# Smaller weight loads, one tanh for two items, evenly spread projections and another start in a one-core attention and MLP kernel

## The chip, the cores and the metric

The kernel runs on one core of one Trainium2 chip. The metric is the device time of one execution in microseconds, as the median of repeated runs. PE is the matrix engine and PEld its weight load, ACT is ScalarE, DVE is VectorE, POOL is GpSimd, SP is the engine that issues the transfers.

## The reference

```python
xn = layernorm(x)                                  # x: 2048 tokens x 1024, bf16
qkv = xn @ wqkv                                    # 32 heads of 32
s = softmax(q @ k.T * 32**-0.5) @ v  -> @ wo       # attention branch
h = gelu_tanh(layernorm(xn) @ w1 + b1)             # w1: 1024 x 3584
g = silu(h @ w2 + b2)                              # w2: 3584 x 1024
out = x + s * g
```

## The kernel before

The attention is cut into 512 units: 8 groups of 4 heads, 8 query blocks of 256, 8 key blocks of 256. A unit is 8 score matmuls, two exps of 128x1024 on ACT, and the value and row-sum matmuls of two units earlier. The MLP (six chunks of at most 352 tokens) and the Q, K and V projections of the next head group are cut into items of about the size that fits into one unit, and each unit takes one item along. All items share one PSUM bank (bank 7), which DVE must empty before the next item can start. The scores have three slots of two banks, and each unit uses two of them, so PE can run ahead of ACT by less than one unit.

```python
while u < NU + 2 or ...:                   # the main loop, cut
    if u < NP: pro_unit(u)                 # the first 8 units: norm, transposes, first projections
    if u < NU: s_unit(u)                   # scores
    for t in act_tasks.pop(u, ()): t()     # tanh of earlier items
    if u < NU: exp_unit(u)                 # two exps
    if 2 <= u < NU + 2: pv_unit(u - 2)
    if u >= NP and state["qi"] < total:    # one item: W1, quarter of W2, K, Q or V
        ...
        for s in it.steps[lo:hi]: s(state["bank"])
        for t in dve_tasks.pop(u, ()): t()             # DVE work of earlier items
        if hi == len(it.steps): it.finish(state["bank"])   # DVE empties the bank
```

A W1 item leaves five operations behind: DVE empties the bank (`xb`), squares and multiplies one and two units later (`u`), and in the third unit ACT takes the tanh and DVE makes `hT`.

```python
            def fin(bk):                                   # w1_item, cut
                op("vector", ... tensor_scalar(xb, bank(bk), b1T ...))
                dve_tasks[u + 1].append(... ub = xb * xb)
                dve_tasks[u + 2].append(... ub = (ub + 1/0.044715) * xb)
                act_tasks[u + 3].append(... th = Tanh(ub))
                dve_tasks[u + 3].append(... hT[:, f] = (th + 1) * xb)
```

The weights come in pieces into two buffers. A W1 piece (4 items) is one transfer of 1 MB, a W2 piece two transfers of 0.75 and 1 MB.

```python
        def load_piece(g):                                 # cut
            s = g % 2
            if k < 7:
                op("sync", ... dma_start(w1v[s], src), w=[("war", s, 0)], dma=f"war{s}")
            else:
                op("sync", ... w2v[s][:, KLO:, :] ..., w=[("war", s, 1)], dma=f"wah{s}")
                op("sync", ... w2v[s][:, 0:KLO, :] ..., w=[("war", s, 0)], dma=f"war{s}")
```

At the start the tokens are taken in pairs of 128-token tiles. `pre_pair` holds the order of the work:

```python
        def pre_pair(p):
            more = p + 1 < NP
            if more: stat(2 * p + 2)       # statistics of a tile of the next pair
            nbias(p)
            xnorm(2 * p); xnorm(2 * p + 1)
            if more: stat(2 * p + 3); rstd(p + 1)
            ycoef(p)
            transp(2 * p); transp(2 * p + 1)
        def pro_unit(p):
            if p + 1 < NP: pre_pair(p + 1) # the next pair ahead of this pair's projections
            if p < 3: ynorm(p)
            pair_kq(p); pair_v(p)
```

The softmax here doesn't subtract the row's maximum and nothing guards it: scores larger than these inputs give would overflow.

## Time and profile before

| | before |
|---|---|
| median (three runs) | 1143.37 us (1141.6 to 1144.8) |
| profiled span | 1140.6 us |
| PE, ACT, DVE busy | 1091.3, 1053.7, 603.6 us |
| from the span's start to the first exp of unit 8 | 65.2 us |
| units 8 to 511 | 1028 us, 2.04 us each |
| after the last exp starts | 47.5 us |

These are lines of the page of before: the busy times, the chain that ended last, and three groups of operations (busy time and mean time of one; then the idle time of the engine just before them and what ended most of it).

```profile
PE 1091.3 (96%) x29952; PEld 695.6 (61%) x29952; DVE 603.6 (53%) x1351; ACT 1053.7 (92%) x1281; POOL 77.0 (7%) x128
...
PE 65%; ACT 27%; DVE 4%; DMA 2%; issue 1%; SPq 0%
...
L635 ACT ACTIVATE P<-ps 128x1024 bf16<-128x1024 f32 x1024 | 986.3, 1102 | 16.0 <-PE ps L623 12.4
...
L409 ACT ACTIVATE th<-u 128x352 f32<-128x352 f32 (+1 forms) x168 | 97.3, 579 | 0.3
```

Two engines are near their limit at once. How near is read from the starts in the timeline, not from busy times, since an ACT operation is shown as busy for longer than it holds up the next one (below, the tanh at 103.23 lasts 0.57 us, but the next exp starts 0.39 us after it). This is ACT in the timeline of before (start, duration, operation), in a stretch where W1 items and projections alternate:

```profile
103.23 0.57 ACT L409 ACTIVATE th<-u 128x352 f32<-128x352 f32 x1
103.62 3.85 ACT L635 ACTIVATE P<-ps 128x1024 bf16<-128x1024 f32 x4
107.23 0.61 ACT L409 ACTIVATE th<-u 128x352 f32<-128x352 f32 x1
```

One tanh and four exps take 4.00 us, two units; a tanh adds about 0.38 us to the 1.81 of two exps. PE needs 2.07 us for a unit with a W1, K or Q item and 1.77 with a V item. So four units W1, K, W1, V cost ACT 8.00 and PE 7.98.

Three kinds of lost time stand out. The first is the start. In the timeline of before, DVE has normalised tiles 0 and 1, and then waits for the rows of tile 4, although tiles 2 and 3 lie ready:

```profile
14.86 1.29 DVE L252 BATCH_NORM_STATS2 stats<-OT 128x6 f32<-128x512 bf16 x2 [3.00 <-DMA OT<-in_A_x_dram]
...
16.45 1.00 DVE L284 TENSOR_SCALAR hT<-OT,lnp 128x1024 bf16<-128x1024 bf16 x2
```

PE in the same stretch transposes tiles 2 and 3 after that, and only then starts the first projections (`xnT,wq`); the first scores (`QT,KT`) start at 23.11 us:

```profile
17.05 1.89 PE L306 MATMUL ps<-ident,hT 128*128 128x128 bf16 x16 [5.34 <-DVE hT L284]
18.87 2.56 PE L315 MATMUL ps<-xnT,wq 128*32 128x256 bf16 x64
21.26 1.92 PE L315 MATMUL ps<-wq,xnT 128*32 128x256 bf16 x64
23.11 0.40 PE L623 MATMUL ps<-QT,KT 32*128 32x256 bf16 x8
```

The second is PE standing still for about a microsecond in the middle of an item, with nothing in the profile that it could wait for ("issue"). The waits of PE between 65 and 1080 us of before (engine, what it was about to do, whom it waited for: total, times, longest):

```profile
PE ps L315 <- issue: 8.2, 11, 1.3
PE ps L315 <- DVE xb L401: 6.5, 15, 0.9
...
PE ps L652 <- issue: 1.6, 4, 0.6
PE ps L623 <- issue: 1.3, 2, 0.8
```

One of them in the timeline: a W2 item stops after 22 of its 28 matmuls.

```profile
186.28 1.06 PE L315 MATMUL ps<-hT,war 128*32 128x352 bf16 x22
188.31 0.48 PE L315 MATMUL ps<-hT,war 128*32 128x352 bf16 x6 [0.97 <-issue]
```

The third is a weight load near 960 us that stands in the queue behind the 2 MB of wo.

### The profile page before, as it was taken

The page shows a single profiled execution, that of the slowest core. Times are in us where ns is not written, and L with a number is a line of the kernel's source. Part 1 is how long each engine was busy: PE and PEld are TensorE (multiplying, and loading weights), DVE is VectorE, ACT ScalarE, POOL GpSimd, SP SyncE. Part 2 cuts the span into 40 slices and gives each one's busy share as a digit, 9 for nine tenths or more (in the row PEclk, how much of TensorE's full clock was granted, in tenths as well). Part 3 has the DMA queues.
Part 4 walks back from the last instruction along what each step waited for, and adds up shares of the span by engine and source line. Part 5 has one row for each costly group of instructions (what it writes and reads, how often), then busy time and mean ns, then how long its engine had stood idle before and what let it go on. Part 6 is the DMA issues. An engine that isn't in the chain of part 4 may idle for free.

```text
span 1140.6 us, 63237 instructions
## 1 busy us (share of the span) xinstructions
PE 1091.3 (96%) x29952; PEld 695.6 (61%) x29952; DVE 603.6 (53%) x1351; ACT 1053.7 (92%) x1281; POOL 77.0 (7%) x128
## 2 busy tenths in 40 slices
PE   4999999999999999999999999999999999899998
PEld 3756655566556665666666665666656565556666
DVE  7457661266672237665226675236585127752378
ACT  3889999999999999999999999999999999899930
POOL 4400000000000000000000000000000000000000
PEclk9999999999999999999999999999999999999999
DMA  9353245322245313224531236412134424443667
GB/s 222 76 169 123 61 114 174 117 80 78 62 129 149 109 43 114 74 72 130 149 104 41 76 107 196 142 61 77 41 105 125 144 90 142 150 133 116 114 172 174
DMA packets 198483, 129.90 MB, mean 114 GB/s; under 512 B 41552, under 2 KB 189008, under 8 KB 198224
## 3 DMA queue, kind: packets, MB, share of 16 engines
q1 hardware_dynamic: 193584, 125.85, 38.2%
q8 instruction: 234, 3.83, 1.4%
q0 software_dynamic: 4640, 0.02, 0.6%
q14 instruction: 25, 0.20, 0.1%
HBM read 104.87 MB, written 12.58 MB: 103 GB/s over the span
## 4 chain that ended last, share of the span: by engine, by line
PE 65%; ACT 27%; DVE 4%; DMA 2%; issue 1%; SPq 0%
PE ps L315 38%; ACT P L635 25%; PE ps L623 10%; PE ps L652 10%; PE ps L655 6%; ACT th L409 2%; DMA war<-in_B_w_dram 1%; DVE xb L401 1%; DMA OT<-in_A_x_dram 1%; DVE u L404 1%; PE ps L306 1%; DVE u L406 0%; DVE hT L413 0%; ACT thz L443 0%; DVE accs L666 0%
## 5 line engine op out<-in xcount | busy, mean ns | idle before, releaser
L635 ACT ACTIVATE P<-ps 128x1024 bf16<-128x1024 f32 x1024 | 986.3, 1102 | 16.0 <-PE ps L623 12.4
L652 PE MATMUL ps<-P,VP 128*32 128x256 bf16 x4096 | 264.1, 278 | 1.6 <-issue 1.6
L655 PE MATMUL ps<-P,ones 128*32 128x256 bf16 x4096 | 258.4, 273 | 1.8 <-issue 1.8
L315 PE MATMUL ps<-yTc,war 128*32 128x352 bf16 (+1 forms) x5376 | 226.6, 309 | 10.7 <-issue 5.1
L315 PE MATMUL ps<-hT,war 128*32 128x352 bf16 (+1 forms) x5376 | 230.1, 308 | 3.6 <-issue 3.1
L623 PE MATMUL ps<-QT,KT 32*128 32x256 bf16 x4096 | 204.6, 273 | 9.8 <-ACT P L635 5.6
L652 PEld LDWEIGHTS ps<-P,VP 128*32 128x32 bf16 x4096 | 108.2, 95 | 110.5 <-issue 98.0
L315 PEld LDWEIGHTS ps<-yTc,war 128*32 128x32 bf16 x5376 | 139.9, 97 | 58.4 <-issue 7.1
L315 PEld LDWEIGHTS ps<-hT,war 128*32 128x32 bf16 x5376 | 141.9, 97 | 45.3 <-issue 5.7
L401 DVE TENSOR_SCALAR xb<-ps,b1T 128x352 f32<-128x352 f32 (+1 forms) x168 | 96.0, 572 | 123.9 <-PE ps L315 122.9
L623 PEld LDWEIGHTS ps<-QT,KT 32*128 32x128 bf16 x4096 | 61.3, 93 | 155.9 <-ACT P L635 88.1
L315 PE MATMUL ps<-xnT,wq 128*32 128x352 bf16 (+2 forms) x3200 | 128.3, 304 | 2.3 <-DVE xb L401 2.1
L675 POOL TENSOR_TENSOR OT<-accs,rcs 128x256 bf16<-128x256 f32 x64 | 53.1, 830 | 1001.7 <-DVE rcs L673 1001.7
L440 DVE TENSOR_SCALAR zh<-ps,b2h 128x352 f32<-128x352 f32 (+1 forms) x48 | 27.5, 573 | 175.5 <-PE ps L315 175.5
L655 PEld LDWEIGHTS ps<-P,ones 128*32 128x32 bf16 x4096 | 110.3, 97 | 4.6 <-issue 3.4
L413 DVE SCALAR_TENSOR_TENSOR hT<-th,xb 128x352 bf16<-128x352 f32 (+1 forms) x168 | 85.7, 510 | 37.7 <-ACT th L409 34.9
L315 PEld LDWEIGHTS ps<-xnT,wq 128*32 128x32 bf16 x3200 | 79.9, 97 | 29.5 <-DVE xb L401 3.2
L409 ACT ACTIVATE th<-u 128x352 f32<-128x352 f32 (+1 forms) x168 | 97.3, 579 | 0.3
L404 DVE TENSOR_TENSOR u<-xb 128x352 f32<-128x352 f32 (+1 forms) x168 | 88.2, 525 | 0.2
L406 DVE SCALAR_TENSOR_TENSOR u<-u,xb 128x352 f32<-128x352 f32 (+1 forms) x168 | 82.9, 494 | 0.1
L315 PE MATMUL ps<-wq,xnT 128*32 128x256 bf16 x2048 | 65.9, 273 | 0.4 <-ACT xnT L309 0.3
L666 DVE COPY accs<-ps 128x256 f32<-128x256 f32 x64 | 27.2, 424 | 67.7 <-PE ps L655 67.7
(44 smaller groups left out, 497.1 us busy)
## 6 DMA issues: line engine op xcount, KB each, us to landing
war<-in_B_w_dram SPq DMA_DIRECT2D x66, 1024.0 KB, 5.6
war<-in_B_w_dram SPq DMA_DIRECT2D x24, 768.0 KB, 5.5
wq<-in_A_wqkv_dram SPq DMA_DIRECT2D x12, 512.0 KB, 5.9
OT<-in_A_x_dram SPq DMA_DIRECT2D x16, 256.0 KB, 6.6
y_scratch<-OT SPq DMA_DIRECT2D x16, 256.0 KB, 2.3
xnT<-in_A_x_dram SPq DMA_DIRECT2D x16, 256.0 KB, 4.1
out_dram<-wq SPq DMA_DIRECT2D x16, 256.0 KB, 2.7
gT_scratch<-gst SPq DMA_DIRECT2D x40, 88.0 KB, 1.7
```

What stands on the lines that cost most here:

```text
L315: ins = e.matmul(outs(j), lhsT=lhs(j), rhs=rhs, start=start, stop=stop, tile_position=(0, 32 * j), skip_group_check=True)
L401: op("vector", lambda e: e.tensor_scalar(xb[:, 0:n], bank(bk, 0, n), b1T[:, f:f + 1], None, op0=ALU.add), r=[("b", bk), "b1"], w=[kx])
L404: "vector", lambda e: e.tensor_tensor(ub[:, 0:n], xb[:, 0:n], xb[:, 0:n], op=ALU.mult), r=[kx], w=[ku]))
L406: "vector", lambda e: e.scalar_tensor_tensor(ub[:, 0:n], ub[:, 0:n], 1.0 / 0.044715, xb[:, 0:n], op0=ALU.add, op1=ALU.mult),
L409: "scalar", lambda e: e.activation(th[:, 0:n], ub[:, 0:n], ACT.Tanh, scale=0.7978845608028654 * 0.044715),
L413: "vector", lambda e: e.scalar_tensor_tensor(hT[:, f, 0:n], th[:, 0:n], 1.0, xb[:, 0:n], op0=ALU.add, op1=ALU.mult),
L440: op("vector", lambda e: e.tensor_scalar(zh[:, 0:n], bank(bk, 0, n), 0.25, b2h[:, nb:nb + 1], op0=ALU.mult, op1=ALU.add), r=[("b", bk), "b ...
L623: ins = e.matmul(bank(bks[j], kh * 256, (kh + 1) * 256), lhsT=KT[i2][32 * j:32 * j + 32, k0:k0 + 128], rhs=QT[i2][32 * j:32 * j + 32, qb * ...
L635: op("scalar", lambda e, p=p, sl=sl: e.activation(pb[:, 2 * p:2 * p + 2, :, :].rearrange("p a b q -> p (a b q)"), ps[:, sl * 1024:(sl + 1) ...
L652: e.matmul(bankq(ACC, j, 0, QW), lhsT=VP[vp][:, kb, vo + 32 * j:vo + 32 * j + 32], rhs=pb[:, j, kh, :], start=first, stop=False, tile_posi ...
L655: ins = e.matmul(bankq(ACC, j, QW, 2 * QW), lhsT=ones[:, 0:32], rhs=pb[:, j, kh, :], start=False, stop=last, tile_position=(0, 32 * j), sk ...
L675: op("gpsimd", lambda e: e.tensor_tensor(OT[:, hg, qb * QW:(qb + 1) * QW], a[:], rc[:], op=ALU.mult), r=[ka, kr], w=[("OT", hg, qb), ("xst ...
```

## The change

The change puts five things together. (1) Weight pieces are loaded in parts of 256 KB with a dependency each, handed to the queue one per unit. (2) Two W1 items share one tanh of 704 columns. (3) The projections are spread over the W1 items by a ratio, not strictly one after each. (4) At the start the rows and weights are loaded in another order, for the first two pairs the statistics come after the normalisation, and the transposes of the second pair come after the first projections. (5) The last multiplication of an attention block moves from POOL to DVE, one unit later.

```diff
-                op("sync", lambda e: e.dma_start(w1v[s], src), w=[("war", s, 0)], dma=f"war{s}")
+        def load_sub(g, q):
+            ...
+                dst, lo, hi = w1v[s], 2 * q, 2 * q + 2      # W2: 4 * q, 4 * q + 4
+            op("sync", lambda e: e.dma_start(dst[:, lo:hi, :], src[:, lo:hi, :]), w=[("war", s, q)], dma=f"war{s}{q}")
+        def load_piece(g):
+            ...
+            for i, q in enumerate(subs):
+                sp_tasks[cur["u"] + i].append((load_sub, g, q))
-                   r=[("war", s, 0), "yTc"], w=[("b", bk)])
+                   r=[("war", s, dc // 2), "yTc"], w=[("b", bk)])
@@ w1_item, fin
-                act_tasks[u + 3].append(... Tanh of th[:, 0:n] <- ub[:, 0:n])
-                dve_tasks[u + 3].append(... hT[:, f] ...)
+                gelu.append((xb, kx, f))
+                if h == 1:
+                    act_tasks[u + 3].append(... Tanh of th[:, :, 0:n] <- ut[:, :, 0:n])
+                    for i, (xq, kq, fq) in enumerate(pair):
+                        dve_tasks[u + 3].append(... hT[:, fq] ...)
@@ order of items
-                take_proj = need and len(flat) >= first_proj and (left - need < 6 or (w1_next and turn))
+                if need and len(flat) >= first_proj and (late or credit >= 1):
@@ start
-            if more:
+            if more and p >= 2:
                 stat(2 * p + 2)
             ...
             if more:
+                if p < 2:
+                    stat(2 * p + 2)
                 stat(2 * p + 3)
+            if 0 < p < NP - 1:
+                transp_pair(p + 1)
             pair_kq(p)
             pair_v(p)
+            if p == 0:
+                transp_pair(1)
@@ pv_unit
-                    op("gpsimd", lambda e: e.tensor_tensor(OT..., a[:], rc[:], op=ALU.mult), ...)
-                dve_tasks[v + 2].append(back)
+                dve_tasks[v + 3].append(lambda: op("vector", lambda e: e.tensor_tensor(OT..., a[:], rc[:], op=ALU.mult), ...))
```

(Cut: the load order at the start, the accounting of the ratio, and the buffers that go with the merged tanh: six `xb` instead of five, two double `u` instead of four single ones, one double `th` instead of two single ones.)

## The prediction

> **What bounds the kernel now.** ScalarE and TensorE are almost balanced. The page gives PE 96% and ACT 92% of 1140.6 us; from 95 to 900 us the window table shows both 98 to 99.8% busy. After a prologue of some 75 us come 504 attention units, each with one piece of MLP or projection work, about 2.04 us a unit. In the timeline the exps follow each other every 0.917 us, so 1.83 us a unit; a unit with a 352-column tanh takes 2.20. PE needs 2.07 us for a unit with a W1 or K/Q item, 1.77 with V, about 1.9 with a W2 part. So W1,K,W1,V costs ACT 8.01 and PE 7.98; W1,Q,W1,Q costs PE 8.28; W1 alone costs ACT 2.20; four W2 parts cost either about 7.7. The last 44 us are PE and DVE work that the change leaves alone.
>
> **1. One tanh for two items.** The Trainium skill ("ScalarE: Activation LUTs", What ACT_TABLE_LOAD costs) gives 186 ns + 0.833 ns per column for an ACTIVATE with immediates, 93 ns of it overlapped: 386 ns for 352 columns. The trace agrees (2.20 - 1.83 = 0.37). A pair would save about 0.09 us, 84 times: 7.5 us of ACT. Most is off the critical path: among projections PE already stands at 7.98. Only W1-only stretches (some 60 units) gain: 2 to 3 us. Against it, the two hT operations (0.44 us each) fall into one unit and wait for a longer tanh, in order ahead of the eviction of the single MLP bank; I estimate 0.1 to 0.3 us of PE wait in every fourth to eighth mixed unit: +3 to +5. POOL's multiplication (0.83 us, 64 times) becomes about 0.35 us each on DVE, 53% busy: little.
>
> **2. Even projections.** The item order shows small shifts: W1:projection goes from 1:1 to between 1:1 and 5:4; runs of Q stay. About 0. Six W1 items instead of four at the start, while DVE still normalises y: +1.
>
> **3. 256 KB parts.** Bytes stay. The chain shows a 12 us wait on a weight load behind the 2 MB of wo near 960 us, which cost ACT 3 to 4 us; finer dependencies should halve it. "Issue" waits of PE of up to 1.3 us (8.4 us on the MLP line) come near 1 MB bursts; W2 parts, freed unit by unit, may save some, W1 parts are still freed within one item. Together -3 to -6.
>
> **4. First token pair.** The chain shows 9.2 us waiting for x rows, until 14.86 us: statistics of tile 4 stand in DVE's order before the normalisation of tiles 2 and 3, and PE transposes these before the first projections. The change moves both and loads V after tiles 4 and 5. First scores should move from 23.1 to about 18 us, and PE's period of 5.5 us carries on: -4.
>
> **Sum:** about -7 us: **1136 us**, 8 in 10 within **1124 to 1147**. Faster by over 2%: 0.08; within 2%: 0.89; slower by over 2%: 0.03.
>
> **What shows it.** Right: first scores near 18 us; 84 tanh with a mean near 0.85 us; ACT busy down by 7 us without an equal fall of the span; more PE waits on DVE's evictions; shorter issue waits in W2 stretches. Wrong: mixed stretches clearly under 2.0 us a unit, or PE waits on DVE over 15 us.
>
> **What would make it wrong.** If buffers let PE or ACT run further ahead than I read, the full 7.5 us counts; if issue waits vanish, up to 10 us more; if bunched DVE work delays every bank, it is slower.

## The result, and the profile after

The changed kernel takes **1134.99 us** (median of four runs, 1134.89 to 1135.25) against 1144.09 us of before in the same rounds. The ratio is 0.9923, 95% interval 0.9905 to 0.9942. A ratio here is always the mean time of one kernel's fast runs over that of the other's of the same rounds, so not quite the ratio of the medians quoted. Between the two profiled runs the span fell by 7.4 us.

The page after, the lines that answer to those of before:

```profile
PE 1093.9 (97%) x29952; PEld 687.1 (61%) x29952; DVE 613.9 (54%) x1415; ACT 1048.2 (92%) x1197; POOL 24.0 (2%) x64
...
PE 63%; ACT 25%; DVE 9%; DMA 2%; issue 1%; SPq 1%
...
L676 ACT ACTIVATE P<-ps 128x1024 bf16<-128x1024 f32 x1024 | 971.5, 1087 | 19.5 <-PE ps L664 11.6
...
L431 ACT ACTIVATE th<-u 128x704 f32<-128x704 f32 (+1 forms) x84 | 66.7, 794 | 0.0
```

ACT is busy for 5.5 us less, but DVE's share of the chain went from 4 to 9%. The start did what was meant: in the timelines of DVE and then of PE, the normalisation of tiles 2 and 3 comes at 12.62 us and the first scores at 18.79.

```profile
12.62 1.00 DVE L285 TENSOR_SCALAR hT<-OT,lnp 128x1024 bf16<-128x1024 bf16 x2
13.54 1.28 DVE L253 BATCH_NORM_STATS2 stats<-OT 128x6 f32<-128x512 bf16 x2
```

```profile
11.34 3.61 PE L316 MATMUL ps<-xnT,wq 128*32 128x256 bf16 x64 [1.27 <-ACT xnT L310]
15.52 2.34 PE L316 MATMUL ps<-wq,xnT 128*32 128x256 bf16 x64 [0.57 <-DMA wq<-in_A_wqkv_dram]
17.79 1.07 PE L307 MATMUL ps<-ident,hT 128*128 128x128 bf16 x16
18.79 0.40 PE L664 MATMUL ps<-QT,KT 32*128 32x256 bf16 x8
```

The waits of PE between 65 and 1080 us after. "Issue" is down to 2.4 us; the casts of the projections' results (Q, K and V) stand further down the same list for the first time, with 2.2, 2.0 and 0.9 us:

```profile
PE ps L316 <- DVE xb L419: 5.6, 21, 0.6
PE ps L664 <- ACT P L676: 3.7, 10, 0.6
PE ps L316 <- issue: 2.4, 3, 1.2
```

ACT in the timeline after, in the stretch shown of before: from tanh to tanh there are now eight exps, four units, and they take 8.24 us where before took 8.00.

```profile
110.32 0.81 ACT L431 ACTIVATE th<-u 128x704 f32<-128x704 f32 x1
111.00 7.70 ACT L676 ACTIVATE P<-ps 128x1024 bf16<-128x1024 f32 x8
118.56 0.81 ACT L431 ACTIVATE th<-u 128x704 f32<-128x704 f32 x1
```

The starts of the exps, two for each unit, give the time of every unit in a trace. Summed by the item that the unit took along (one profiled run each, "mixed" is everything with or next to a projection, "W1 only" a W1 item between W1 items):

| stretch | units | before, us | after, us | difference |
|---|---|---|---|---|
| start to the first exp of unit 8 | 8 | 65.2 | 59.8 | -5.4 |
| units 8 to 23 | 16 | 34.4 | 36.5 | +2.1 |
| mixed and W1 only | 257 | 529.3 | 536.4 | +7.1 |
| W2 parts | 192 | 379.1 | 371.2 | -7.9 |
| W1 and Q of the last chunk, round wo's load | 27 | 61.7 | 58.3 | -3.4 |
| the rest | | 70.9 | 71.0 | +0.1 |

So the total of -7.4 us is a gain of 16.7 us (start, W2, last chunk) of which 9.2 us are given back in the W1 and projection stretches. My prediction had named these places, but which part of the change does which, and how much, the sums do not show.

### The profile page after: what moved, and what is told of

Read it like the earlier page. It is cut to its first block, busy times and chain, and to the rows that moved or that the text cites. A ratio compares the mean times of both kernels' runs of the same rounds, so it can differ in the third digit from the quotient of the medians.

```text
span 1133.2 us, 63275 instructions
## 1 busy us (share of the span) xinstructions
PE 1093.9 (97%) x29952; PEld 687.1 (61%) x29952; DVE 613.9 (54%) x1415; ACT 1048.2 (92%) x1197; POOL 24.0 (2%) x64
## 3 DMA queue, kind: packets, MB, share of 16 engines
q8 instruction: 234, 3.83, 1.4%
## 4 chain that ended last, share of the span: by engine, by line
PE 63%; ACT 25%; DVE 9%; DMA 2%; issue 1%; SPq 1%
PE ps L316 38%; ACT P L676 22%; PE ps L664 10%; PE ps L693 9%; PE ps L696 6%; DVE hT L436 3%; ACT th L431 2%; DVE xb L419 1%; DVE u L422 1%; DMA war<-in_B_w_dram 1%; DMA wq<-in_A_wqkv_dram 1%; DVE u L424 1%; DVE accs L707 1%; DVE trs L708 1%; ACT thz L466 0%
## 5 line engine op out<-in xcount | busy, mean ns | idle before, releaser
L676 ACT ACTIVATE P<-ps 128x1024 bf16<-128x1024 f32 x1024 | 971.5, 1087 | 19.5 <-PE ps L664 11.6
L316 PEld LDWEIGHTS ps<-yTc,war 128*32 128x32 bf16 x5376 | 133.8, 96 | 71.9 <-DVE xb L419 11.0
L436 DVE SCALAR_TENSOR_TENSOR hT<-th,xb 128x352 bf16<-128x352 f32 (+1 forms) x168 | 79.5, 508 | 26.8 <-ACT th L431 26.1
L422 DVE TENSOR_TENSOR u<-xb 128x352 f32<-128x352 f32 (+1 forms) x168 | 84.2, 501 | 0.8
L431 ACT ACTIVATE th<-u 128x704 f32<-128x704 f32 (+1 forms) x84 | 66.7, 794 | 0.0
L316 PE MATMUL ps<-xnT,OT 128*32 128x352 bf16 (+1 forms) x1536 | 58.0, 308 | 0.4 <-DVE wq L509 0.4
```

The costliest lines, as they stand in the source:

```text
L316: ins = e.matmul(outs(j), lhsT=lhs(j), rhs=rhs, start=start, stop=stop, tile_position=(0, 32 * j), skip_group_check=True)
L422: "vector", lambda e: e.tensor_tensor(ub[:, 0:n], xb[:, 0:n], xb[:, 0:n], op=ALU.mult), r=[kx], w=[ku]))
L431: "scalar", lambda e: e.activation(th[:, :, 0:n], ut[:, :, 0:n], ACT.Tanh, scale=0.7978845608028654 * 0.044715),
L436: "vector", lambda e: e.scalar_tensor_tensor(hT[:, fq, 0:n], th[:, i, 0:n], 1.0, xq[:, 0:n], op0=ALU.add, op1=ALU.mult),
L676: op("scalar", lambda e, p=p, sl=sl: e.activation(pb[:, 2 * p:2 * p + 2, :, :].rearrange("p a b q -> p (a b q)"), ps[:, sl * 1024:(sl + 1) ...
```

## The experiments

Twelve kernels were built and run, all with five rounds, all correct. The letters: a_ is one part alone on the kernel before; b_ is several parts; p_ and t_ are variants of the parts and of the tanh.

| kernel | what it is | median, us | before, us | ratio (95%) |
|---|---|---|---|---|
| (changed) | all five parts | 1134.99 | 1144.09 | 0.9923 (0.9905 to 0.9942) |
| a_start | start alone | 1137.18 | 1145.01 | 0.9929 (0.9911 to 0.9948) |
| a_parts | 256 KB parts alone | 1128.51 | 1145.01 | 0.9855 (0.9833 to 0.9877) |
| a_tanh | one tanh for two alone | 1154.05 | 1145.01 | 1.0086 (1.0059 to 1.0113) |
| a_proj | even projections alone | 1147.91 | 1145.01 | 1.0025 (1.0005 to 1.0045) |
| p_burst | parts, not spread over units | 1130.26 | 1146.07 | 0.9856 (0.9838 to 0.9873) |
| p_dep | parts, one dependency for all | 1130.88 | 1146.42 | 0.9862 (0.9841 to 0.9883) |
| t_spread | a_tanh, second hT a unit later | 1150.86 | 1146.07 | 1.0038 (1.0019 to 1.0057) |
| t_two | a_tanh with two tanh in a row (flawed) | 1174.38 | 1146.07 | 1.0248 (1.0228 to 1.0268) |
| t_two2 | the same, mended | 1153.69 | 1146.42 | 1.0063 (1.0039 to 1.0087) |
| b_sp | start and parts | 1124.67 | 1146.07 | 0.9805 (0.9788 to 0.9822) |
| b_notanh | the change without the merged tanh | 1125.42 | 1146.42 | 0.9813 (0.9787 to 0.9839) |
| b_best | b_sp, tanh merged in W1-only stretches | 1124.97 | 1146.42 | 0.9811 (0.9787 to 0.9836) |

### One part at a time

Each edit is the hunks of that part from the diff above, applied to the kernel before.

a_start, expected:

> The kernel before with the new start alone (load order, statistics after normalisation, transposes of the second pair after the first projections). My theory: the gain of the start is kept to the end, first scores near 18.8 us as in the changed kernel, 4 to 5.5 us faster in all, so about 1139. Rival: what is gained at the start is lost again at the first wait for a weight load or for the buffers of the first W1 items, so under 2 us.

Measured: ratio 0.9929, about 8 us, more than I expected. The gain is kept. In its trace unit 8 begins 2.6 us and the last exp 5.4 us earlier than in before. What comes later is not the start's: its W2 parts took 2.4 us less, with 8 instead of 10 of the instruction stops described below, and its trace has no stretch of half clock, which before's has for 3.4 us (both below). Runs of before differ by up to 6 us among themselves, so the median has some chance in it. The rival falls.

a_parts, expected:

> The kernel before with 256 KB parts alone. My theory: W2 stretches lose their issue stalls (mean W2 unit 1.973 us before, 1.926 in the changed kernel), the wo wait shrinks: 4 to 8 us faster, about 1137 to 1140. Rival: those stalls are chance in one profile, and the timed runs move by less than 2 us.

Measured: ratio 0.9855, about 16.5 us, twice the most that I expected and the largest part of the change. The rival, chance, falls.

a_tanh, expected:

> The kernel before with one tanh for two W1 items alone. My theory: ScalarE does 5 to 7 us less, but PE waits for DVE's bunched evictions, so the time moves between -2 and +4 us. Rival: ScalarE is the bound, all counts, 5 to 7.5 us faster.

Measured: ratio 1.0086, about 10 us **slower**. Both expectations missed; mine (-2 to +4 us) allowed for the direction, but not for the size. ACT has less to do, yet the time goes up: the rival, that ACT's total decides, falls. The changed buffer counts are not what costs, as far as the list of waits shows: ACT waits for no release by DVE in a_tanh, and for 0.3 us in t_spread.

a_proj, expected:

> The kernel before with evenly spread projections alone. My theory: within 2 us of before, since the order hardly changes and both engines are balanced in either order. Rival: even spreading removes runs in which PE or ScalarE alone is the bound, 3 us or more faster.

Measured: ratio 1.0025, about 3 us slower and barely clear of zero, so neither expectation holds. The order does hardly change. In the second head group, for one, the items stand as follows before and after (W is W1, 2 a quarter of W2):

```
before 222222222222222222222222kWvWkWvWkWvWkWvWkWvWkWvWqWvWqWvqqqqWWWWW
after  222222222222222222222222WkWvWkWvkWvWkWvWkvWkWvWqWvqWvWqWqqqWWWWW
```

The four ratios add to -1.05% (-0.71, -1.45, +0.86, +0.25), where the whole change has -0.77%. The fifth part was not run alone.

### Why 256 KB parts help

The edit of p_burst, on a_parts:

```diff
-                sp_tasks[cur["u"] + i].append((load_sub, g, q))
+                load_sub(g, q)
```

> As a_parts (256 KB parts, each with its own dependency), but all parts of a piece are put into the DMA queue at once where the piece's load stood, not one per unit. Theory A, pacing: it is the 1 MB burst in front of PE's instruction fetch that stalls PE, so a burst of four small parts stalls it as before: issue waits of PE back to some 10 us, time 1140 or more. Theory B, size and dependency: small transfers let the fetch in between, or parts are released one by one by their readers, whatever the order in the queue: about as a_parts, 1126 to 1131.

Measured: ratio 0.9856, the same as a_parts with 0.9855. Spreading the parts over the units adds nothing. For the W1 pieces it was never in effect: the four parts of one become free together, and so they go out in one burst in a_parts too, as here in its timeline (in p_burst they take 1.91 us as well):

```profile
121.87 1.91 SPq L370 DMA_DIRECT2D war<-in_B_w_dram  x4
```

Of the W2 pieces, a_parts spreads some over several units, and p_burst puts the seven parts of each out as one group, within 3.0 to 6.2 us. So it isn't bursts as such that stall PE. The edit of p_dep, on a_parts:

```diff
-                   r=[("war", s, dc // 2), "yTc"], w=[("b", bk)])
+                   r=[("war", s, q) for q in range(4)] + ["yTc"], w=[("b", bk)])
-                   r=[("war", s, f // 4), ("hT", f)], w=[("b", bk)])
+                   r=[("war", s, q) for q in range(7)] + [("hT", f)], w=[("b", bk)])
```

> As a_parts (ratio 0.9855), 256 KB parts, but every matmul that reads a piece waits for all its parts, and so a load waits for the last reader of the whole piece, as before. Theory size: small transfers alone remove the stalls, so 1127 to 1131 (ratio 0.984 to 0.988). Theory dependency: loads freed part by part are what spreads them, so 1135 or more (ratio above 0.990).

Measured: ratio 0.9862, again the same. The finer dependency is worth next to nothing; it is the size of one transfer that counts, as far as these runs reach. One combination was not run: small parts at once and with one dependency for all. The W1 pieces come near to it in every one of these kernels; some of the W2 pieces are still spread a little in each, by the pacing or by the dependency.

What small transfers remove is seen in the waits of PE between 65 and 1080 us of a_parts. "Issue" on the MLP line fell from 8.2 to 2.4 us, and the issue waits before the scores and the value matmuls are gone from the list (its first three lines):

```profile
PE ps L315 <- DVE xb L415: 7.0, 16, 0.9
PE ps L637 <- ACT P L649: 5.3, 20, 0.4
PE ps L315 <- issue: 2.4, 4, 0.9
```

The trace also holds the packets of the queue that brings PE its instructions (q8 on the page: 234 packets, 3.83 MB, so 16 KB each). The Trainium skill ("Runtime: NRT & Kernel Launch", Instruction fetch mechanics) says that each engine fetches its program in 16 KB blocks of 256 instructions over a queue of its own; this agrees: PE's 59,904 matmuls and weight loads are 234 times 256, and in before 88 other instructions of PE come on top. I took every place between 65 and 1075 us where two successive PE instructions (matmuls or weight loads) of one and the same group start over 0.85 us apart, and looked for the last packet of that queue that had ended before PE went on. In before there are 10 such stops, 11.7 us together, and in **every** one PE goes on 1.23 to 1.60 us after a packet's end. Over thirteen kernels (all but t_two) there are 69, each 1.20 to 1.60 us after one. Kernels with the large loads have 8 to 10 such stops (before, a_start, a_tanh, a_proj, t_spread, t_two2), kernels with 256 KB parts 1 to 3 (a_parts, p_burst, p_dep, b_sp, b_notanh, b_best, and the changed kernel). So PE was waiting for its instructions. The trace holds a second proof of it: if all instructions of PE are counted in the order of their starts, the number that started before the stop leaves the same remainder, 193, in division by 256, for all 76 stops of the fourteen kernels. PE stops at one and the same place of a block, where the next block has to be there.

These blocks came late while weights were loaded. In before, the last packet ahead of a stop started 6.3 to 8.7 us after the packet before it, where the median is 4.5, and in the 4 us ahead of it the queue that carries the weights (q1) had moved over 0.9 MB in all ten cases. That is true of 66 of the 211 packets of this stretch, so a stop goes with such a load, but such a load does not always bring a stop. And the volume alone does not make the stop: in p_burst 52 of 214 packets follow such a stretch, and there are 2 stops.

Why the size of one transfer, and not the bytes in the queue, makes them late, the runs do not show. The Trainium skill has a candidate: on the page "DMA: Bandwidth & Descriptors", Queues, rings and completion order, each DMA engine goes round its queues by whole packets of up to 64 descriptors, so that a fetch would wait for the end of the other queue's packet. That a 1 MB load makes larger packets than a 256 KB load is my guess; the page does not say it, and no run here measured it. It stays argued.

The last chunk gains too. The 27 units round wo's load took 61.7 us in before and 58.7 in a_parts. The wait for the weight load behind wo fell from 12.0 to 9.7 us. Right after that wait, from 972.5 us on, the trace of before records half the clock for 3.4 us, which is worth about 1.7 us at most (an estimate: half of 3.4). The profiled runs of the kernels with large loads have such a stretch of 3.4 or 6.8 us between 972 and 1006 us, all but a_start; those with 256 KB parts have none there. What starts it the runs do not show.

So of the 13.2 us between the profiled spans of before and a_parts some 9.5 are instruction stops (11.7 against 2.2 us), and most of the rest is this wait and the half clock. The timed gain of 16.5 us holds some more of the latter: the mean clock of before's eleven runs is 0.997, that of a_parts' four 1.000, by which I estimate 3 us (0.3% of 1145).

### Why the merged tanh costs

ACT in the timeline of a_tanh, with W1 items and projections alternating:

```profile
104.17 0.79 ACT L416 ACTIVATE th<-u 128x704 f32<-128x704 f32 x1
104.85 7.90 ACT L643 ACTIVATE P<-ps 128x1024 bf16<-128x1024 f32 x8
112.64 0.79 ACT L416 ACTIVATE th<-u 128x704 f32<-128x704 f32 x1
113.32 7.61 ACT L643 ACTIVATE P<-ps 128x1024 bf16<-128x1024 f32 x8
120.81 0.79 ACT L416 ACTIVATE th<-u 128x704 f32<-128x704 f32 x1
```

Four units take 8.47 and 8.17 us instead of 8.00. In the starts of the exps the usual four units W1, V, W1, K take 2.50, 1.81, 1.88 to 2.08, and 2.07 us: the unit with the tanh goes at ACT's pace, the last two at PE's. Over the 227 mixed units a_tanh took 473.3 us, before 462.7.

There are two explanations. DVE: both `hT` operations now wait for a longer tanh, in one unit, and stand in DVE's order ahead of the operation that empties the MLP bank. ACT bunching: one unit of four holds all of the tanh work, and PE, with less than a unit of score buffers, cannot use the slack of that unit in the next. The waits of PEld in a_tanh, between 65 and 1080 us, show that the first is real: the wait for V's cast (9.3 us) is not in before's list at all.

```profile
PEld ps L315 <- DVE xb L404: 13.1, 32, 0.8
...
PEld ps L315 <- DVE VP L351: 9.3, 35, 0.7
```

The edit of t_spread, on a_tanh (the last pair of a chunk is left as it was, because the W2 items need it):

```diff
-                        dve_tasks[u + 3].append(lambda i=i, xq=xq, ...
+                        dve_tasks[u + 3 + (i if f < FB - 1 else 0)].append(lambda i=i, xq=xq, ...
```

> As a_tanh (one tanh for two W1 items, 1154.05), but the second hT operation of a pair one unit later, so that DVE never has both in one unit. Theory DVE: bunched hT work holds up the bank's evictions and casts, so this recovers most: 1146 or less. Theory ScalarE bunching: one unit of four carries both tanh (2.5 us) and PE cannot run ahead to make use of the other units' slack, so it stays at 1150 to 1156.

Measured: ratio 1.0038, a median within the second expectation, but by the ratios a little over half of the loss is recovered. The mixed units take 465.4 us (a_tanh 473.3, before 462.7), and the wait for V's cast is down to 0.3 us. But the pattern is mostly still 2.50, 1.81, 1.81, 2.06, or 8.18 us (the median of the 34 stretches W1, V, W1, K or Q; in before it is 8.02, in a_tanh 8.34). ACT's share of the pattern would be 7.92 (four times 1.81 and 0.68, the time from the tanh's start to the next exp's), PE's 7.98; neither is reached, since the two units 2.50 and 1.81 go at ACT's pace and the unit of 2.06 at PE's.

t_two was to test the bunching with ACT's total of before:

```diff
-                    act_tasks[u + 3].append(... Tanh of th[:, :, 0:n])
+                    for i in range(2):
+                        act_tasks[u + 3].append(... Tanh of th[:, i, 0:n], w=[kt])
```

> As a_tanh, but two separate 352-column tanh in that same unit: the same total of ScalarE work as before, bunched. Theory ScalarE bunching: the unit takes 2.58 instead of 2.50 us and the others stay bound by PE, so 4 to 8 us slower than a_tanh: 1158 to 1162. Theory DVE: the first hT can start 0.3 us earlier than after the merged tanh, so about 1148 to 1154.

Measured: ratio 1.0248, far outside both. The edit is at fault: both tanh are recorded as writers of one tile, so the kernel's own bookkeeping makes the second wait for the end of the first. In the trace 0.99 us pass from the first tanh to the next exp, where the merged one needs 0.68. The run says nothing about the question. t_two2 gives each half its own record (`w=[kt + (i,)]`):

> t_two again, mended: there the second tanh waited for the end of the first, since both were recorded as writers of one tile; here each has its own record. ScalarE's total is that of before, bunched in one unit of two W1 items. Theory ScalarE bunching: units of 2.58 us instead of 2.50, the others as in a_tanh: 4 to 8 us slower than a_tanh (ratio 1.012 to 1.016). Theory DVE alone: as a_tanh or faster (ratio up to 1.009).

Measured: ratio 1.0063, as a_tanh (1.0086) or a little better, outside what I had expected from bunching and inside what I had expected from DVE alone. The tanh unit is longer, 2.60 instead of 2.50, but the next W1 unit is shorter, 1.81 instead of 1.88 to 2.08; that DVE gets its first half earlier would explain it. Yet the waits of PE and PEld between 65 and 1080 us show that DVE alone is not the cause here. These are those of t_two2 for the exps and for V's cast:

```profile
PE ps L632 <- ACT P L644: 15.6, 52, 1.7
PEld ps L315 <- DVE VP L351: 1.2, 2, 0.6
```

In a_tanh they were 3.0 and 9.3 us. The wait for DVE is nearly gone, and PE waits for ACT instead. So t_two2 shows what the bunching of ACT's work costs, with the amount of before: the 34 stretches have a median of 8.27 us against 8.02. Merging takes 0.09 off that (t_spread, 8.18), and both `hT` in one unit add 0.16 (a_tanh, 8.34). These are one trace each; by the times, two tanh in one unit cost the same merged or not, to within the intervals. What costs is the place of the work, both tanh and both `hT` in one unit, not its amount.

### What a better version keeps

b_sp takes the start and the parts only, b_notanh undoes the merged tanh in the changed kernel.

> The kernel before with the new start and the 256 KB parts, without the merged tanh, the even projections and the multiplication on DVE. If the parts of the change add up, 7.8 (start) and 16.5 us (parts) go together: about 1121, some 14 us below the whole changed kernel (1135.0). Rival: the start and the parts remove partly the same stalls (the stall of unit 2 is gone in both), so 1124 to 1128.

> The changed kernel with one tanh for each W1 item again (start, parts, even projections and the multiplication on DVE stay). If the merged tanh is what costs, as it cost 9 us alone, this takes 1126 to 1129 against 1135 for the whole change; the rest to b_sp (ratio 0.9805) is then the even projections and the multiplication, 2 to 4 us. Rival: in the changed order the merged tanh is harmless, and it stays at 1133 to 1136.

Measured: 0.9805 and 0.9813. b_sp gains 1.95%, about 22 us, where its two parts alone gave 2.16%; its median lies at the lower end of the rival's range, so they may share a little, though the intervals do not settle that. b_notanh lies just under its range, and 1.1% below the whole change by the ratios (9.6 us by the medians, of different rounds); the rival, that the merged tanh is harmless there, falls. The even projections and DVE's multiplication, which are all that b_notanh has over b_sp, cost nothing that these intervals can tell, so the 2 to 4 us that I had put down to them are not seen. In b_notanh's timeline two units, from tanh to tanh, take 4.00 us again, so four take 8.00:

```profile
105.92 0.50 ACT L424 ACTIVATE th<-u 128x352 f32<-128x352 f32 x1
106.30 3.77 ACT L668 ACTIVATE P<-ps 128x1024 bf16<-128x1024 f32 x4
109.92 0.54 ACT L424 ACTIVATE th<-u 128x352 f32<-128x352 f32 x1
```

b_best merges the tanh only where the next item is a W1 item too:

```diff
+                more = h == 0 and f < FB - 1 and state["qi"] < len(flat) and flat[state["qi"]][0].w1
-                if h == 1:
+                if not more:
```

> b_sp (start and parts) with a merged tanh only where two W1 items follow each other without a projection between, and their two hT operations in different units. There ScalarE is the bound (2.20 us a unit against 2.07 of PE), so some 30 pairs save 0.08 us each: 1 to 3 us faster than b_sp, ratio about 0.978. Rival: even there the bunching costs as much as it saves, ratio 0.980 or more.

Measured: 0.9811, not to be told from b_sp. The 27 units of the last chunk fell from 58.8 to 57.7 us, which is too little to show in the time; the rival (0.980 or more) holds. Both b_sp and b_best beat the kernel before and the changed kernel; b_sp is the simpler one.

## Why the prediction was right or wrong

The sum was right (1136 predicted, 1134.99 measured), but that it came out so near is luck: the terms have errors of about 10 us that cancel, too little gain for the parts and too little loss for the merged tanh. Point by point:

- **Balance of ACT and PE.** Right. A part that takes work off ACT alone (5.5 us of busy time in the changed kernel) does not shorten the kernel; alone it lengthens it.
- **1, merged tanh ("+3 to +5" against "2 to 3 us" of gain).** The mechanism was right in kind: DVE's bunched `hT` work holds up the eviction and the casts, as t_spread and the PEld waits show. The size was off: about +10 us alone, and 10 to 13 in the whole change (b_notanh against the change). The missed half is the bunching of ACT's own work: I added up four units and found ACT at 7.9 and PE at 7.98, and took the larger as the cost. With less than one unit of buffers the cost is nearer the sum of the larger of the two in each part of the pattern: t_spread, with the `hT` work apart, still takes 8.18 us for four units. By the traces of t_two2, t_spread and a_tanh (8.27, 8.18 and 8.34 us against 8.02), ACT's bunching is about 0.25 us of four units, DVE's 0.16, and merging gives back 0.09. The mean of the merged tanh is 0.794 us, not 0.85.
- **2, even projections ("About 0", and +1 for the six first W1 items).** Alone about +3 us, at the edge of the interval; in the time of b_notanh not to be seen. Units 8 to 23 took 2.1 us longer in the change and in b_notanh (36.5 against 34.4) and 0.9 in a_proj (35.3), so the +1 was right in kind; the rest of b_notanh makes up for most of it.
- **3, 256 KB parts ("-3 to -6").** This is the most mis-sized term: -16.5 us alone. I had seen that issue waits come near 1 MB bursts, but argued that W1 parts, still freed within one item, would burst as before. They do burst, four parts within 1.9 us in the timeline of a_parts, and yet PE's stops went from 10 to 2. That is the step that failed: what stalls PE is the size of one transfer, not the burst, and neither pacing nor the finer dependency, on which I had counted, matters (p_burst, p_dep).
- **4, start ("-4").** 4.3 us for the first scores (18.79 us, about 18 predicted); 5.4 us by unit 8 in the change, 2.6 in a_start; about 8 us in the ratio of a_start, of which fewer stops and the clock are part.
- **5, the multiplication on DVE ("little").** Not tried alone; together with the projections it costs nothing visible in b_notanh.

## What to carry to other kernels

When two engines are balanced and the buffers between them hold less than one step, count the larger of the two in each step, not the larger of the two sums; work that is merged, but thereby bunched into one step, cost more here than the merging saved. Look at unexplained stops of an engine with a long straight-line program beside its instruction-fetch packets, and count whether the stops fall at one place of a block of 256 instructions: here, cutting 1 MB loads to 256 KB took most of them away, with the same bytes and the same burst. And run each part of a compound change alone: here two parts gained 22 us and one gave back 10 or more.

## What the Trainium skill lacked or had wrong

- "Runtime: NRT & Kernel Launch", Instruction fetch mechanics, calls crossing a 16 KB block "mostly hidden". The blocks agree with the trace (234 packets, 3.83 MB), and most crossings are hidden here too, but not all: of the 211 packets between 65 and 1075 us of before, 10 go with a stop of PE of 0.86 to 1.61 us inside a group of like instructions, each ending 1.23 to 1.60 us after such a packet and each at the same place of a block of 256 instructions.
- No page that I read says that the size of one data transfer decides this: with 256 KB parts 1 to 3 stops and a ratio of 0.9855 are left, whether the parts are queued one per unit or at once (0.9856). "DMA: Bandwidth & Descriptors", Queues, rings and completion order, gives the arbitration by packets from which it might follow.
- "ScalarE: Activation LUTs", What ACT_TABLE_LOAD costs, agrees: 186 ns + 0.833 ns per column less 93 ns makes, as an estimate, 0.386 us for 352 columns and 0.68 for 704; the traces have about 0.38 and 0.68 from the tanh's start to the next exp's. For the exps it comes out a little high: 0.946 us for 1024 columns by the same sum, where two exps took 1.81 us, 0.905 each.
